# Fused dilated attention, Fourier mixing and FFN: five early FFN tiles, four weight tiles ahead, one key buffer, full-height transform matmuls

## The chip, the cores and the metric

One core of one Trainium2 chip. The time is the device time of one execution in microseconds (us); lower is better. The engines are TensorE (PE, with its weight loads shown apart as PEld), VectorE (DVE), ScalarE (ACT), GpSimd (POOL) and SyncE (SP, which issues most transfers).

## The reference

Attention over 8 batches of 576 tokens with 8 heads of 64, a causal window of 32 for half of the heads and a dilated one (every fourth key of 128) for the others; then a real Fourier mix over tokens and channels, a normalisation, and a two-layer FFN of 512 to 2048 to 512 with a residual.

```python
scores = scale * np.matmul(q, k.transpose(0, 1, 3, 2))
scores = np.where(masks[None], scores, -1e9)        # plain window / dilated window
attn = softmax(scores); x = np.matmul(attn, v)      # laid out as (8, 576, 512)
mixed = np.real(np.fft.fft(np.fft.fft(x, axis=1), axis=2))
u = x + mixed
un = (u - mean(u)) / np.sqrt(var(u) + 1e-6)
out = u + np.maximum(un @ w_ch1, 0.0) @ w_ch2       # float64 weights, 512x2048 and 2048x512
```

## The kernel before, in words

Every operation is recorded with a cost, a priority and the buffers that it touches (class `Plan`); a greedy list scheduler then writes each engine's instructions out in a fixed order. So an engine runs its list in order, and a number in the program can change the order everywhere.

- **Attention** (`attention`, `attend`): batch by batch, four pairs of heads each, three units a pair: scores (L536), mask and maximum on DVE (L544), exponent on ACT (L550), transposes (L563), values (L570). Queries and keys are transposed on DVE into `tq` and `tk` (L511), two buffers each; ACT copies `tk` into `kb` (L522).
- **Mix** (`mix`): the two transforms as matmuls with high and low parts: along the tokens (L752, its last piece with 97 or 33 rows in `eot` and `tail_sb`; the edge column at L774), along the channels (L798) with one matmul of 34 rows (`ye`, `alt_sb`, L804). Rows are normalised, written to DRAM (`us`) and read back transposed (`tokens`).
- **Weights** (`prep`): the float64 weights of one FFN tile f (128 of the 2048 hidden units) come as two loads, and DVE (L874 to L883, four instructions a load), ACT and POOL (L886) make high and low float32 parts of them. The first NF1 tiles (`wa`) are made during attention and staged in the ring `ut` of NUT = 3 buffers, in which the transposed token blocks also live and in which buffers are given out in the order of the program text: all `wa` stages stand ahead of the first token block. When attention is over its memory is freed, and NFA more tiles (`wb`) are made through a ring `wst` of two; the others follow when the mix memory is freed.
- **FFN**: tokens go in 9 chunks of 512 (8 of the batches, one of left-over rows). `fill` does the first few tiles of a chunk **early**, while attention and mix of later batches run, in blocks of 256 tokens: up (L900, `ut`, 256 columns) for each tile, then down (L916), and the partial sum goes to DRAM (`part`). Before the change chunks 0 to 8 have 4, 4, 4, 4, 3, 3, 3, 2, 0 early tiles. When the mix is done, the **late loop** runs chunk by chunk over the remaining tiles with 512 columns: 24 matmuls a tile, 12 up and 12 down (`utwbb` and `utlate` are its token blocks, `hh` its hidden values, whose low part DVE makes at L908).

Priorities: attention comes first, then mix, then weight tiles (8 + 8f), and `fill` last (1000 and more), so early tiles are what TensorE does when it has nothing else.

Of the kernel before, what the change touches and what calls it, by code (L numbers as in the profile page):

```python
# [9 lines left out]
F32 = mybir.dt.float32  # L10
# [9 lines left out]
P = 128  # L20
KT = C // P
NF = FF // P
NF1 = 4
N4 = 4
N2 = 1
TOK = 4 * P
TOK1 = 2 * P
NX = 4
NUT = 3
NUC = 2  # L30
NH = 4
NLATE = 4
NPE = 1
LO1 = 'DVE'
NFA = 2
P_QK0, P_V0 = -8.0, -7.0
P_ST, P_FD, P_WD, P_ST0, P_FD0, P_SPAN0, P_SPAN1 = -4.0, -12.0, -10.0, 0.0, 0.0, 8.0, 13.0
P_QK, P_V, P_TR, P_MIX, P_SPAN, P_W, P_WF, P_FILL, P_FILLT = -8.0, -7.0, -5.0, 2.0, 13.0, 8.0, 8.0, 45.0, 4.0
# [24 lines left out]
def tables():  # L63
    def split(t):
        hi = round12(t)
        return np.stack([hi, round12(t - hi)], axis=1).astype(np.float32)

    def turn(a, b, n, kind):
        k = np.outer(np.arange(a), np.arange(b)) % n
        ang = 2.0 * np.pi * k / n  # L70
        if kind == "cos":
            t = np.cos(ang)
            t[(4 * k == n) | (4 * k == 3 * n)] = 0.0
        else:
            t = np.sin(ang)
            t[(k == 0) | (2 * k == n)] = 0.0
        return t

    def pad(t, rows, cols):
        out = np.zeros((rows, cols))  # L80
        out[: t.shape[0], : t.shape[1]] = t
        return out

    seq = np.stack([split(pad(turn(NSH, NSH, S, kd), 3 * P, NSP)) for kd in ("cos", "sin")])
    seq = seq.reshape(2, 3, P, 2, NSP)
    tail = np.zeros((P, 3, NSP), np.float32)
    for r in (0, 64):
        tail[r:r + 33, 0] = seq[0, 2, :33, 0]
    for r in (64, 96):
        tail[r:r + 32, 1] = seq[1, 2, :32, 0]  # L90
    tail[0:33, 2] = seq[0, 2, :33, 1]
    tail[32:64, 1] = seq[1, 2, :32, 1]
    seq = seq[:, :2]
    ch = np.stack([split(pad(turn(2 * P, NEH, C, kd), 2 * P, NEP)) for kd in ("cos", "sin")])
    ch = ch.reshape(2, 2, P, 2, NEP)
    alt = np.zeros((34, NEP), np.float32)
    sign = 0.5 * (1.0 - 2.0 * (np.arange(NEH) % 2))
    for r in (0, 1, 32, 33):
        alt[r, :NEH] = sign
    q = np.arange(QB)[:, None]  # L100
    j = np.arange(KB)[None, :]
    band = (j > q) & (j <= q + WIN)
    first = band & (j >= WIN)
    cross = band & ((q < 48) | (j >= WIN + 48))
    mask = np.where(np.stack([band, first, cross], 1), 0.0, NEG).astype(np.float32)
    eye = np.eye(P, dtype=np.float32)
    rest = np.arange(P).reshape(4, 32)
    rest[1::2] = rest[1::2, ::-1]
    ident = np.stack([eye, eye[:, ::-1], eye[:, rest.reshape(-1)]], axis=1)
    n = np.arange(QB)  # L110
    orders = (
        np.concatenate([n[:72], n[:71:-1]]),
        np.concatenate([n[47::-1], n[48:]]),
        np.concatenate([n[:24], n[:23:-1]]),
    )
    perm = np.stack([eye[:QB, o] for o in orders], axis=1)
    flip = np.arange(P, dtype=np.int32)[::-1].reshape(P, 1)
    flip = np.concatenate([flip, rest.reshape(P, 1).astype(np.int32)], axis=1)
    flip = (flip[:, :, None] + P * np.arange(4, dtype=np.int32)).reshape(P, 8)
    return dict(  # L120
        seq=np.ascontiguousarray(seq),
        tail=tail,
        chn=np.ascontiguousarray(ch),
        alt=alt,
        mask=np.ascontiguousarray(mask),
        ident=np.ascontiguousarray(ident),
        perm=np.ascontiguousarray(perm),
        flip=np.ascontiguousarray(flip),
    )
# [211 lines left out]
def fused_kernel(ctx: ExitStack, tc, q, k, v, w1, w2, seq, tail, chn, alt, mask, ident, perm, flip, out):  # L341
# [30 lines left out]
    def attw(tag, shape, dtype=F32, bufs=2):  # L372
        return plan.buf(lambda: pools["att"], tag, shape, dtype, bufs)
# [4 lines left out]
    def fixed(pool_, shape, dtype, name):  # L378
        return Buf(ap=pool_.tile(shape, dtype, name=name))
# [11 lines left out]
    tail_sb = fixed(keep, [P, 3, NSP], F32R, "tail_sb")  # L391
    eot = fixed(keep, [P, 2, NEH], F32R, "eot")
    chn_sb = [fixed(keep, [P, 2, 2, NEP], F32R, f"chn{i}") for i in range(2)]
    alt_sb = fixed(keep, [34, NEP], F32R, "alt_sb")
    ye = fixed(keep, [34, NSP], F32R, "ye")
    half = fixed(keep, [P, 1], F32, "half")
    kbs = [fixed(heads, [P, 2, WIN + S], F32, f"kb{i}") for i in range(2)]
    vts = [fixed(heads, [P, 4, 6, D + 1], F32, f"vt{i}") for i in range(2)]
# [10 lines left out]
    def start():  # L409
        dma(lambda: nc.sync.dma_start(out=mask_sb(), in_=mask), (), (mask_sb,), -9, QB * 3 * KB * 4)  # L410
        dma(lambda: nc.sync.dma_start(out=ident_sb(), in_=ident), (), (ident_sb,), -8, P * 3 * P * 4)
        dma(lambda: nc.sync.dma_start(out=perm_sb(), in_=perm), (), (perm_sb,), -7, QB * QB * 12)
        dma(lambda: nc.sync.dma_start(out=flip_sb(), in_=flip), (), (flip_sb,), 50, P * 32)

        def zero(t, eng, cost, fn, key=None, prio=-5.0):
            add(eng, cost, fn, (), ((t, key) if key is not None else t,), prio)

        zero(half, "DVE", 0.07, lambda: nc.vector.memset(half(), -0.5))
        for n, t in enumerate(kbs):
            for e in range(2):  # L420
                def clear(t=t, e=e):
                    ps = slice(64 * e, 64 * e + 64)
                    nc.vector.memset(t()[ps, 1 - e], 0.0)
                    nc.vector.memset(t()[ps, e, 0:WIN], 0.0)
                zero(t, "DVE", 0.8, clear, ("z", e), -6.0 + n)
        for i, t in enumerate(vts):
            def ones(t=t, i=i):
                nc.gpsimd.memset(t()[:, :, :, D:D + 1], 1.0)
                for blk in ((0,), (0, 3))[i]:
                    nc.gpsimd.memset(t()[0:WIN, :, blk, 0:D], 0.0)  # L430
            zero(t, "POOL", 1.0, ones)
        for t in xs + xtail:
            zero(t, "DVE", 0.07, lambda t=t: nc.vector.memset(t()[:, C:C + 1], 0.0), "pad")
        zero(eot, "DVE", 0.2, lambda: nc.vector.memset(eot().bitcast(F32)[32:64, 0], 0.0), ("gap", 0))
        zero(eot, "DVE", 0.2, lambda: nc.vector.memset(eot().bitcast(F32)[0:32, 1], 0.0), ("gap", 1))
        zero(ye, "DVE", 0.2, lambda: nc.vector.memset(ye().bitcast(F32), 0.0))
        for b in range(B):
            dma(lambda b=b: nc.sync.dma_start(
                out=xsm[b]()[0:1], in_=kbs[0]()[0:1, 1, WIN:WIN + C],
            ), ((kbs[0], ("z", 0)),), ((xsm[b], "zero"),), 12 * b + 6, 2048)  # L440
        for i in range(2):
            for m in range(2):
                add("POOL", 0.06, lambda i=i, m=m: nc.gpsimd.dma_start(out=seq_sb[i]()[:, m], in_=seq[i, m]),
                    (), ((seq_sb[i], m),), 6 + i, P * 2 * NSP * 4, at=T_SEQ + i)
                add("POOL", 0.06, lambda i=i, m=m: nc.gpsimd.dma_start(out=chn_sb[i]()[:, m], in_=chn[i, m]),
                    (), ((chn_sb[i], m),), 9 + i, P * 2 * NEP * 4, at=T_CHN + i)
        add("POOL", 0.06, lambda: nc.gpsimd.dma_start(out=tail_sb(), in_=tail), (), (tail_sb,), 6.5, P * 3 * NSP * 4, at=T_SEQ + 0.5)
        add("POOL", 0.06, lambda: nc.gpsimd.dma_start(out=alt_sb(), in_=alt), (), (alt_sb,), 8, 34 * NEP * 4, at=T_SEQ + 4)

# [49 lines left out]
    def attend_pair(b, dil, j, staged, xts, when):  # L501
        p0 = when(0) + P_TR

        def transposed(name):
            t = attw("t" + name, [P, S])

            def go():
                o = t()[:, :]
                if dil:
                    o = t().rearrange("p (r n a) -> p n a r", r=DIL, n=18, a=8)  # L510
                nc.vector.transpose(  # L511
                    out=o, in_=staged[name]()[:, 18 * j:18 * j + 18].rearrange("p n d -> p (n d)")
                )
            add("DVE", 0.67, go, (staged[name],), (t,), p0)
            return t

        tq = transposed("q")
        kb = kbs[j]
        tk = transposed("k")
        for e in range(2):  # L520
            ps = slice(64 * e, 64 * e + 64)
            add("ACT", act(S), lambda e=e, ps=ps: nc.scalar.copy(out=kb()[ps, e, WIN:], in_=tk()[ps]),  # L522
                (tk,), ((kb, e),), p0)
        for u in range(3):
            attend(b, dil, j, u, tq, kb, xts[u], when(u))
# [145 lines left out]
    def mix(b, when):  # L671
# [59 lines left out]
        def pieces(i):  # L731
# [5 lines left out]
            def tail_of(cols):  # L737
                if i:
                    return [(eot()[:, 1, cols], tail_sb()[:, 1])]
                return [(eot()[r, 0, cols], tail_sb()[r, c]) for r, c in ((slice(0, 97), 0), (slice(0, 33), 2))]  # L740
            return [(((src, m),), (seq_sb[i], m), 3, whole(m)) for m in range(2)] + [
                (((eot, "eo"[i]), (eot, ("gap", i))), tail_sb, 2 - i, tail_of)]

# [296 lines left out]

    def early(c):

        if c == NCH - 1:
            return 0
        return NF1 if c < N4 else NF1 - 2 if c >= B - N2 else NF1 - 1

    def fill(ut, tiles):
        prio = P_FILL + tiles[0] * P_FILLT
# [113 lines left out]
```

## Time and profile before

| | |
|---|---|
| median of 3 runs | 1205.33 us (1204.33 to 1207.46) |
| the profiled execution | 1203.13 us, span 1201.4 us |
| TensorE clock granted, mean over the span | 0.975 of full |
| PE / DVE / ACT / POOL busy | 1119.6 / 638.5 / 456.1 / 298.5 us |
| matmuls | 5932 |
| transfers | 132.83 MB, mean 111 GB/s |

The span runs from the first to the last instruction; the profiled execution lasts 1.7 us longer than its span. Busy times of different engines overlap. A matmul of one group overlaps the next, so its mean duration is longer than the distance from one start to the next, and work is costed below by that distance.

### The profile page before, as it was taken

The page shows a single profiled execution, that of the slowest core. Times are in us where ns is not written, and L with a number is a line of the kernel's source. Part 1 is how long each engine was busy: PE and PEld are TensorE (multiplying, and loading weights), DVE is VectorE, ACT ScalarE, POOL GpSimd, SP SyncE. Part 2 cuts the span into 40 slices and gives each one's busy share as a digit, 9 for nine tenths or more (in the row PEclk, how much of TensorE's full clock was granted, in tenths as well). Part 3 has the DMA queues.
Part 4 walks back from the last instruction along what each step waited for, and adds up shares of the span by engine and source line. Part 5 has one row for each costly group of instructions (what it writes and reads, how often), then busy time and mean ns, then how long its engine had stood idle before and what let it go on. Part 6 is the DMA issues. An engine that isn't in the chain of part 4 may idle for free.

```text
span 1201.4 us, 17217 instructions
## 1 busy us (share of the span) xinstructions
PE 1119.6 (93%) x5932; PEld 917.6 (76%) x5932; DVE 638.5 (53%) x1993; ACT 456.1 (38%) x1036; POOL 298.5 (25%) x351
## 2 busy tenths in 40 slices
PE   3887999998999899988889999999999999999998
PEld 2666877787888787866767888888888888888886
DVE  4798888979886868759952231314132231411211
ACT  3785767667574735334332120212112121211210
POOL 1135454544333344414431010202001020110100
PEclk9788899999999999989899999999999999999999
DMA  9978869997777345463642130504031050400201
GB/s 204 218 172 155 165 147 158 219 168 149 155 176 158 91 115 183 123 201 123 173 124 72 38 103 1 141 1 123 18 88 53 2 139 1 123 18 1 88 1 36
DMA packets 284183, 132.83 MB, mean 111 GB/s; under 512 B 204998, under 2 KB 255528, under 8 KB 284096
## 3 DMA queue, kind: packets, MB, share of 16 engines
q1 hardware_dynamic: 280752, 123.22, 45.1%
q0 software_dynamic: 2960, 7.99, 2.4%
q8 instruction: 47, 0.77, 0.3%
q10 hardware_dynamic: 384, 0.52, 0.1%
q14 instruction: 40, 0.33, 0.1%
HBM read 94.94 MB, written 36.75 MB: 110 GB/s over the span
## 4 chain that ended last, share of the span: by engine, by line
PE 67%; DVE 14%; DMA 7%; SPq 4%; issue 3%; POOL 2%; ACT 2%; DVEq 0%; ACTq 0%; POOLq 0%
PE ff L900 26%; PE mix L916 9%; PE sc L916 8%; PE sc L536 4%; PE pt L916 4%; PE av L916 4%; DMA ut<-us 4%; PE av L570 3%; PE mix L752 3%; DVE ut L1007 2%; PE mix L798 2%; PE pt L563 2%; SPq L492 1%; DVE pm L544 1%; SPq L997 1%
## 5 line engine op out<-in xcount | busy, mean ns | idle before, releaser
L908 DVE SCALAR_TENSOR_TENSOR hh<-ff,hh 128x512 fp32r<-128x512 f32 x117 | 80.5, 688 | 389.6 <-ACT hh L906 389.6
L906 ACT ACTIVATE hh<-ff 128x512 fp32r<-128x512 f32 x117 | 69.8, 597 | 379.1 <-PE ff L900 378.8
L900 PE MATMUL ff<-utwbb,wb 128*128 128x512 f32 x720 | 181.0, 401 | 9.8 <-POOL wb L886 7.3
L900 PEld LDWEIGHTS ff<-utwbb,wb 128*128 128x128 f32 x720 | 138.8, 194 | 42.7 <-POOL wb L886 8.7
L550 ACT ACTIVATE pm<-pm,mx 96x128 f32<-96x128 f32 x384 | 132.0, 394 | 44.6 <-DVE mx L544 41.7
L900 PE MATMUL ff<-utlate,wb 128*128 128x512 f32 x576 | 139.9, 392 | 0.0
L536 PE MATMUL sc<-kb,tq 128*96 128x256 f32 x384 | 112.0, 408 | 22.9 <-ACT kb L522 20.6
L960 POOL DMA_INDIRECT ut<-us,flip_sb x20 | 19.5, 975 | 449.3 <-DMA out_dram<-ut 347.6
L900 PEld LDWEIGHTS ff<-utlate,wb 128*128 128x128 f32 x576 | 108.1, 188 | 24.2
L916 PE MATMUL sc<-wb,hh 128*128 128x512 f32 x432 | 111.9, 392 | 4.1 <-DVE hh L908 4.1
L916 PE MATMUL mix<-wb,hh 128*128 128x512 f32 x432 | 110.8, 391 | 0.3 <-DVE hh L908 0.2
L544 DVE CUSTOM_DVE_ANT_0 pm<-sc,mask_sb 96x128 f32<-96x128 f32 x384 | 94.5, 276 | 20.7 <-PE sc L536 15.4
L570 PEld LDWEIGHTS av<-vt,ptsb 128*96 128x96 f32 x768 | 79.7, 172 | 25.8 <-issue 7.1
L916 PEld LDWEIGHTS sc<-wb,hh 128*128 128x128 f32 x432 | 80.8, 188 | 23.6 <-DVE hh L908 5.7
L570 PE MATMUL av<-vt,ptsb 128*96 128x65 f32 x768 | 85.7, 256 | 11.6 <-DVE xt L582 8.7
L916 PEld LDWEIGHTS mix<-wb,hh 128*128 128x128 f32 x432 | 81.0, 188 | 18.6 <-DVE hh L908 0.5
L536 PEld LDWEIGHTS sc<-kb,tq 128*96 128x96 f32 x384 | 58.3, 177 | 35.0 <-ACT kb L522 20.8
L900 PE MATMUL ff<-ut,wa 128*128 128x256 f32 x528 | 80.3, 297 | 4.0 <-DVE h L908 4.0
L1007 DVE STREAM_TRANSPOSE ut<-ut 128x512 f32<-128x512 f32 (+1 forms) x68 | 66.6, 1020 | 32.1 <-DMA ut<-us 24.9
L900 PEld LDWEIGHTS ff<-ut,wa 128*128 128x128 f32 x528 | 70.5, 196 | 7.2 <-DVE h L908 4.8
L916 PE MATMUL ff<-wa,h 128*128 128x512 f32 x264 | 70.4, 407 | 0.7 <-ACT h L906 0.5
L916 PE MATMUL pt<-wb,hh 128*128 128x512 f32 x216 | 61.1, 391 | 0.0
(152 smaller groups left out, 1731.1 us busy)
## 6 DMA issues: line engine op xcount, KB each, us to landing
us<-uc SPq DMA_DIRECT2D x36, 257.0 KB
st<-in_q_dram SPq DMA_DIRECT2D x64, 144.0 KB
st<-in_k_dram SPq DMA_DIRECT2D x64, 144.0 KB
ut<-in_w_dram SPq DMA_DIRECT2D x18, 512.0 KB
ut<-us SPq DMA_DIRECT2D x36, 256.0 KB
part<-row SPq DMA_DIRECT2D x32, 256.0 KB
ut<-part SPq DMA_DIRECT2D x32, 256.0 KB
ut<-us SPq DMA_DIRECT2D x56, 128.0 KB
```

The source lines that it names most:

```text
L536: nc.tensor.matmul(sc()[:QB, 256 * n:256 * n + 256], lhsT=tq()[:, cols], rhs=kb()[:, :, keys], start=True, stop=True,)
L544: nc.vector.tensor_tensor_reduce(pm()[:, i], sc()[:QB, KB * i:KB * i + KB], mask_sb()[:, masks[blocks[i // 2]]], -0.125, 3.0e38, ALU.add, ...
L550: add("ACT", 0.295, lambda i=i: nc.scalar.activation(out=pm()[:, i], in_=pm()[:, i], func=AF.Exp, bias=mx()[:, i:i + 1], scale=-1.0), ((mx ...
L563: nc.tensor.transpose(ps()[:, QB * i:QB * i + QB], pm()[:, i], order)
L570: add("PE", 0.16, lambda i=i: nc.tensor.matmul(av()[:QB, 65 * i:65 * i + 65], lhsT=pt()[:, i], rhs=vts[dil]()[:, j + 2 * (i % 2), blocks[i ...
L752: nc.tensor.matmul(ps()[:, :NSP], lhsT=lt, rhs=tab, start=(m == 0 and n == 0), stop=(m == 2 and n == count - 1),)
L798: nc.tensor.matmul(ps()[:n, :NEP], lhsT=ys[i]()[:, dt, a, rows], rhs=chn_sb[i]()[:, dt, c], start=(dt == 0 and x == 0), stop=(i == 1 and d ...
L900: nc.tensor.matmul(z()[:, :n_tok], lhsT=wf()[:, a, kk], rhs=ut()[:, p, kk], start=(kk == 0 and n == 0), stop=(kk == KT - 1 and n == 2),)
L906: add("ACT", act(n_tok) - 0.05, lambda: nc.scalar.activation(out=h()[:, 0, :n_tok], in_=z()[:, :n_tok], func=AF.Relu), (z,), ((h, 0),), prio)
L908: add("DVE", dve(n_tok), lambda: nc.vector.scalar_tensor_tensor(h()[:, 1, :n_tok], z()[:, :n_tok], 0.0, h()[:, 0, :n_tok].bitcast(F32), op ...
L916: nc.tensor.matmul(acc(), lhsT=h()[:, a, P * s:P * s + P], rhs=wf()[:, p], start=(first and n == 0), stop=(last and n == 2),)
L1007: nc.vector.transpose(out=o[back], in_=x[:, g])
```

## The change

Chunks 0 to 8 get 5, 5, 5, 5, 4, 4, 4, 3, 0 early tiles (35 in place of 27). Five weight tiles instead of four are made during attention (NF1), with five buffers for hidden values (NH). Four instead of two further tiles are made after attention and before the mix memory is freed (NFA). `tk` has one buffer. `eot`, `ye`, `alt_sb` are used at their full 128 rows, with zeros in the rows that held nothing.

```diff
-NF1 = 4
-N4 = 4
-N2 = 1
+NF1 = 5
+NE = (5, 5, 5, 5, 4, 4, 4, 3, 0)
-NH = 4
+NH = 5
-NFA = 2
+NFA = 4
...
-    alt = np.zeros((34, NEP), np.float32)
+    alt = np.zeros((P, NEP), np.float32)
...
-    alt_sb = fixed(keep, [34, NEP], F32R, "alt_sb")
-    ye = fixed(keep, [34, NSP], F32R, "ye")
+    alt_sb = fixed(keep, [P, NEP], F32R, "alt_sb")
+    ye = fixed(keep, [P, NSP], F32R, "ye")
...
-        zero(eot, "DVE", 0.2, lambda: nc.vector.memset(eot().bitcast(F32)[32:64, 0], 0.0), ("gap", 0))
+        def gaps():
+            for r in (32, 96):
+                nc.vector.memset(eot().bitcast(F32)[r:r + 32, 0], 0.0)
+        zero(eot, "DVE", 0.4, gaps, ("gap", 0))
...
-            t = attw("t" + name, [P, S])
+            t = attw("t" + name, [P, S], F32, 2 if name == "q" else 1)
...
-                return [(eot()[r, 0, cols], tail_sb()[r, c]) for r, c in ((slice(0, 97), 0), (slice(0, 33), 2))]
+                return [(eot()[:, 0, cols], tail_sb()[:, c]) for c in (0, 2)]
...
-        if c == NCH - 1:
-            return 0
-        return NF1 if c < N4 else NF1 - 2 if c >= B - N2 else NF1 - 1
+        return NE[c]
```

Lines after the first edits are numbered 2 higher in the changed program (L900 is L902 there).

The change also moves the order of the engines' lists. First, TensorE's list of before around its first early up matmuls (`ff<-ut,wa_0` with 256 columns); 58 of the 192 score matmuls stand ahead of them.

```order
L651 MATMUL mix<-ident_sb,uc 128x128 x4
L570 MATMUL av<-vt_154,ptsb 96x65 x4
L536 MATMUL sc<-kb_153,tq 96x256
L563 MATMUL pt<-ident_sb,pm 128x96
L536 MATMUL sc<-kb_153,tq 96x256
L563 MATMUL pt<-ident_sb,pm 128x96 x2
L900 MATMUL ff<-ut,wa_0_132 128x256 x9
L563 MATMUL pt<-ident_sb,pm 128x96 x2
L900 MATMUL ff<-ut,wa_0_132 128x256 x3
L900 MATMUL ff<-ut,wa_1_133 128x256 x3
```

The same place of the change: TensorE's list around its first early up matmuls.

```order
L538 MATMUL sc<-kb_155,tq 96x256 x2
L653 MATMUL mix<-ident_sb,uc 128x128 x4
L572 MATMUL av<-vt_157,ptsb 96x65 x2
L653 MATMUL mix<-ident_sb,uc 128x128 x4
L572 MATMUL av<-vt_157,ptsb 96x65 x2
L565 MATMUL pt<-perm_sb,pm 128x96 x4
L538 MATMUL sc<-kb_155,tq 96x256 x2
L565 MATMUL pt<-perm_sb,pm 128x96 x4
L902 MATMUL ff<-ut,wa_0_132 128x256 x3
L572 MATMUL av<-vt_157,ptsb 96x65 x4
```

72 of the 192 score matmuls stand ahead of the first early up matmul now, that is exactly three batches of attention. Up to the last score matmul of the third batch the list had 48 early up matmuls and 137 transform matmuls; it has 0 and 75 now. Up to the last value matmul of all (L570) it had 339 up and 168 down matmuls of the early tiles, and has 423 and 210; behind it stood 309 and 156, and stand 417 and 210.

Second, POOL's list of the change where it makes the low parts of the last early weight tiles (`wa_3`, second half, and both halves of `wa_4`; `t`, `ees`, `oos`, `eot` are those of the second batch's mix).

```order
L705 TENSOR_TENSOR t_1714<-xt_163,xt_162 33x257
L888 TENSOR_TENSOR wa_3_140<-ut,wa_3_140 128x512
L725 TENSOR_TENSOR eot<-ee,eot 33x257
L727 TENSOR_TENSOR eot<-oo,eot 32x256
L888 TENSOR_TENSOR wa_4_136<-ut,wa_4_136 128x512
L888 TENSOR_TENSOR wa_4_141<-ut,wa_4_141 128x512
L668 TENSOR_TENSOR x_158<-x_158,dm 128x257
```

In the list of before the second half of `wa_3` is the last of the early tiles and stands directly behind the same two `eot` rows. The two halves of `wa_4` now follow them, ahead of the rows in which a mix adds its result (`x`, `dm`).

Third, TensorE's list of before where the late loop begins (chunk 0, tiles 4, 5, 6, 7; `sc`, `pt`, `av` are its sums).

```order
L900 MATMUL ff<-utwbb,wb_4_6204 128x512 x3
L900 MATMUL ff<-utwbb,wb_5_6206 128x512 x3
L916 MATMUL sc<-wb_4_6205,hh 128x512 x6
L916 MATMUL pt<-wb_4_6205,hh 128x512 x3
L916 MATMUL av<-wb_4_6205,hh 128x512 x3
L900 MATMUL ff<-utwbb,wb_6_7215 128x512 x12
L916 MATMUL sc<-wb_5_6207,hh 128x512 x6
```

The same place of the change.

```order
L918 MATMUL sc<-wb_5_6380,hh 128x512 x6
L918 MATMUL pt<-wb_5_6380,hh 128x512 x3
L918 MATMUL av<-wb_5_6380,hh 128x512 x3
L902 MATMUL ff<-utwbb,wb_7_6383 128x512 x12
L918 MATMUL sc<-wb_6_6382,hh 128x512 x6
L918 MATMUL pt<-wb_6_6382,hh 128x512 x3
L918 MATMUL av<-wb_6_6382,hh 128x512 x3
L902 MATMUL ff<-utwbb,wb_8_6385 128x512 x12
L918 MATMUL sc<-wb_7_6384,hh 128x512 x6
L918 MATMUL pt<-wb_7_6384,hh 128x512 x3
L918 MATMUL av<-wb_7_6384,hh 128x512 x3
L902 MATMUL ff<-utwbb,wb_9_7628 128x512 x12
```

Before, tile 6 is the first that is made after the mix memory is freed, and it is the third of chunk 0; now that is tile 9, the fifth of chunk 0.

## Rows read from the trace of the kernel before

**Rows 1.** The page, busy time (share), instructions of each engine.
```profile
PE 1119.6 (93%) x5932; PEld 917.6 (76%) x5932; DVE 638.5 (53%) x1993; ACT 456.1 (38%) x1036; POOL 298.5 (25%) x351
```
**Rows 2.** Stages: length, then busy (instructions) by engine, clock, DMA, GB/s.
```profile
core 0: us, PE busy (x) PEld busy (x) DVE busy (x) ACT busy (x) POOL busy (x), PEclk, DMA share, GB/s
51.50:99.00 47.50, 37.71 (x231) 28.10 (x229) 41.02 (x185) 38.58 (x98) 15.07 (x16) 0.87 0.90 193
99.00:159.80 60.80, 56.10 (x387) 46.84 (x387) 51.03 (x206) 38.46 (x97) 29.57 (x39) 0.91 0.68 129
159.80:426.80 267.00, 250.49 (x1757) 210.03 (x1756) 221.68 (x980) 174.34 (x458) 106.16 (x147) 0.99 0.78 161
426.80:528.50 101.70, 94.26 (x599) 81.19 (x597) 72.28 (x180) 40.73 (x91) 40.90 (x53) 1.00 0.54 150
528.50:532.20 3.70, 1.42 (x5) 0.86 (x5) 2.88 (x3) 1.84 (x4) 0.00 (x0) 0.73 0.39 140
532.20:618.40 86.20, 74.61 (x289) 57.61 (x290) 75.87 (x99) 35.59 (x61) 44.01 (x29) 0.91 0.48 147
618.40:1195.70 577.30, 577.02 (x2521) 472.76 (x2519) 143.44 (x202) 100.79 (x167) 53.63 (x47) 1.00 0.21 57
```
**Rows 3.** Timeline of PE, one early block: start, us, instructions.
```profile
508.64 1.58 PE L900 MATMUL av<-ut,wa 128*128 128x256 f32 x12
510.06 1.65 PE L900 MATMUL pt<-ut,wa 128*128 128x256 f32 x12
511.55 4.36 PE L916 MATMUL sc<-wa,h 128*128 128x512 f32 x18
515.75 1.58 PE L900 MATMUL pt<-ut,wa 128*128 128x256 f32 x12
```
**Rows 4.** Waits of PE from 524 to 640 us: total, times, longest.
```profile
PE ff L900 <- POOL wb L886: 7.3, 3, 4.7
PE sc L916 <- DVE hh L908: 4.1, 4, 3.0
```
**Rows 5.** Timeline of PE, chunk 0 of the late loop, with idle time before.
```profile
532.20 8.32 PE L900 MATMUL ff<-utwbb,wb 128*128 128x512 f32 x24 [2.28 <-ACT utwbb L1024]
...
573.44 4.89 PE L900 MATMUL ff<-utwbb,wb 128*128 128x512 f32 x11 [4.68 <-POOL wb L886]
...
586.37 2.88 PE L900 MATMUL ff<-utwbb,wb 128*128 128x512 f32 x12
...
608.70 4.37 PE L900 MATMUL ff<-utwbb,wb 128*128 128x512 f32 x11 [2.01 <-POOL wb L886]
```
**Rows 6.** The page's groups: count, busy us, mean ns, idle before.
```profile
L908 DVE SCALAR_TENSOR_TENSOR hh<-ff,hh 128x512 fp32r<-128x512 f32 x117 | 80.5, 688 | 389.6 <-ACT hh L906 389.6
```
**Rows 7.** Timeline of PE in the last mix, short and full last pieces.
```profile
467.82 1.38 PE L752 MATMUL mix<-tail_sb,eot 97*128 97x290 f32 x4
469.13 1.67 PE L916 MATMUL ff<-wa,h 128*128 128x512 f32 x6
...
473.71 0.97 PE L752 MATMUL mix<-seq,oos 128*128 128x290 f32 x6
474.52 0.30 PE L752 MATMUL mix<-tail_sb,eot 128*128 128x290 f32 x1
```
**Rows 8.** Groups of PE by shape, the short ones.
```profile
L752 PE MATMUL mix<-tail_sb,eot 97*128 97x290 f32 x16 | 6.6, 410 | 1.6 <-POOL eot L723 1.4
L804 PE MATMUL mix<-alt_sb,ye 34*128 34x258 f32 x16 | 6.1, 383 | 0.0
```
**Rows 9.** Groups of PEld by shape, the same piece at full and short height.
```profile
L752 PEld LDWEIGHTS mix<-tail_sb,eot 128*128 128x128 f32 x16 | 3.0, 190 | 0.0
L752 PEld LDWEIGHTS mix<-tail_sb,eot 97*128 97x128 f32 x16 | 3.0, 190 | 3.6 <-POOL eot L723 2.4
```
**Rows 10.** Timeline of PE, the first early up matmuls.
```profile
125.88 2.01 PE L900 MATMUL ff<-ut,wa 128*128 128x256 f32 x9
```
**Rows 11.** Timeline of POOL, the last early weight tile done.
```profile
151.24 1.28 POOL L886 TENSOR_TENSOR wa<-ut,wa 128x512 fp32r<-128x512 f32 x1 [8.62 <-ACT wa L885]
```
**Rows 12.** Groups of ACT by shape, copies out of the key buffer.
```profile
L522 ACT COPY kb<-tk 64x576 f32<-64x576 f32 x64 | 42.8, 669 | 28.7 <-DVE tk L511 18.5 <-DVE rinv L581 3.9 <-DVE sums L578 2.5
```

More of the change, by code (lines that the diff above doesn't have):

```diff
@@ L447, in start @@
         add("POOL", 0.06, lambda: nc.gpsimd.dma_start(out=tail_sb(), in_=tail), (), (tail_sb,), 6.5, P * 3 * NSP * 4, at=T_SEQ + 0.5)
-        add("POOL", 0.06, lambda: nc.gpsimd.dma_start(out=alt_sb(), in_=alt), (), (alt_sb,), 8, 34 * NEP * 4, at=T_SEQ + 4)
+        add("POOL", 0.06, lambda: nc.gpsimd.dma_start(out=alt_sb(), in_=alt), (), (alt_sb,), 8, P * NEP * 4, at=T_SEQ + 4)
     def load_v(b, dil, prio):
```

## The prediction

> **What bounds the kernel now.** The page's first part comes first: TensorE is busy in 93% of the span and no other engine in more than 53% [rows 1]. An average over stages hides where the rest is, so the next view is the table of stages [rows 2]. Its first two stages lie in attention (before 51.5 us stand the start and the first batch), the third ends with the scores of the last batch, the fourth with the last early tile, then come chunk 0 of the late loop and chunks 1 to 8. In the last stage TensorE is busy for 577.0 of 577.3 us at full clock, so nothing but TensorE sets its length: 105 tiles, 5.50 us each. Chunk 0 is another matter: 12 tiles take 86.2 us in place of 66.0, at a clock of 0.91, while VectorE is busy for 75.9 us. Between 159.8 and 528.5 us TensorE has 344.7 of 368.7 us. The waits near chunk 0 [rows 4] name POOL's weight parts (7.3 us) and VectorE's low parts of the hidden values (4.1 us), and the timeline [rows 5] shows where: the first up matmuls run cold (8.32 us for 24, in a stage after one at clock 0.73), the fifth tile that is made there waits 4.68 us, the tenth 2.01 us.
>
> **Tiles moved from late to early.** Eight chunk-tiles go from the late loop (117 to 109) to the early blocks (27 to 35). Late, one costs 5.50 us (above). Early, 12 up matmuls of 256 columns start 1.42 us after one another and 18 down matmuls take 4.20 us, 0.233 each [rows 3]; a block of 256 tokens needs 12 up and 6 down for a tile, 2.82 us, and a chunk two blocks, 5.64 us. So 45.1 us are added before 528.5 us and 44.0 us taken away after it: **+1.1 us**. That halving the columns nearly halves the time is what makes the move free, and also what makes it worthless by itself: the early phase is bound by TensorE as well, so it becomes longer by about what the late loop loses. By the counts of the order, 84 up and 42 down of these land before the end of attention, 108 and 54 behind it.
>
> **Chunk 0 of the late loop.** Ten tiles were made after the mix memory was freed, seven are now, and four instead of two stand ready. VectorE's 75.9 us there, less 11 low parts of 0.69 us [rows 6], leave 68.3 us for ten tiles (and four short transposes), 6.8 a tile, with 5.50 on TensorE: the tile that VectorE makes can't keep up with the one that TensorE eats, and the lead decides. Before, the fifth made tile was ready 41.2 us after the start at 532.2, the seventh no later than 54.2, the tenth after 76.5 [rows 5]. Now the first up needs 2.9 us extra for the cold clock as before, and the fifth made tile is wanted after 2.9 + 8 x 5.5 = 46.9 us, the seventh and last after 57.9. Both are there, by 5.7 and 3.7 us. So of 20.2 us lost (86.2 - 66.0) the cold start stays and some 2 us of small waits: 5 left, **-15 us**. Bounds: all but the cold start goes, -17; or VectorE is late for the last three tiles by what it was late for the last three before, and the gain is 8.
>
> **Two more tiles ahead, one more early.** Their VectorE work, 6.8 us a tile, goes into 426.8 to 528.5 us (two) and into attention (one). In the former VectorE is idle for 29.4 us and that stage grows by 25 us of early tiles, so TensorE covers it; without the cover the two would cost 13.6 us. Their loads meet DMA at 0.54 there, and SP's list is not what that stage waits for. **+1 us** for hidden values queued behind them on VectorE (0 to 6).
>
> **Full-height matmuls.** In the last mix [rows 7] four short pieces take 1.31 us to the next start, 0.33 each, while six full ones of the same 290 columns take 0.81 us, 0.135 each. The short one also spoils the next: the six down matmuls behind it take 1.67 us. There are 16 pieces of 97 rows and 16 of 33, and 16 + 8 channel matmuls of 34 rows [rows 8], besides 16 edge pieces of one column. 32 x 0.19 is 6.2 us; the 24 lose about 0.18 (wide ones last 0.08 us longer than full pieces of 290 columns, for 32 columns less) and as much as half of that behind them, 6 us; the edge some 1.5. That is 14 us at most on TensorE, of which part lies in stalls that stay: **-12 us**, 5 to 14. What the extra rows hold is zero, and the table that grows by 94 rows is loaded once.
> The weight loads themselves do not differ: 190 ns at 97 rows and at 128 [rows 9]. The Trainium skill, "TensorE: Matmul & The Clock Gate", section "LDWEIGHTS (loading the stationary operand)", says just this, that a load's time goes by columns and not by the contracted rows; the trace agrees, and by that rule alone padding would give nothing. The Trainium skill, "TensorEngine Tiling (Array Packing)", section "Key Properties", says on the other hand that a change of tiling mode, not of the tile alone, drains TensorE; the trace looks like that [rows 7], since the cost is in the distance between starts. I go by the distance.
>
> **The start of the early tiles.** This is the price. The ring of three `ut` buffers is given out in the order of the program, all weight stages first, so a fifth early tile stands between the ring and the first token block, with a later priority than attention's third batch. Before, the first early up ran at 125.88 us [rows 10], the last early tile being ready only after 151.24 us [rows 11]; now 14 more score matmuls go ahead of it, those that ran up to 159.8. By the order 48 up and 62 transform matmuls leave the stretch 99.0 to 159.8 us: 48 x 0.118 + 62 x 0.135 = 14.0 us of TensorE. Attention without that work is not paced by TensorE: in the stretch ahead one batch took 47.5 us with TensorE busy 37.7 at clock 0.87 and VectorE 41.0. A little over half of the transforms stay, so the stretch shrinks from 60.8 not to 47.5 but to about 54.5. 14.0 us of work are put off and 6.3 us come back: **+8 us**. Bounds 0 (it shrinks by all of it) and 14 (not at all).
>
> **One buffer of transposed keys.** The second pair's transpose waits until ACT has copied the first pair's, two copies of 0.67 us [rows 12]. In the order other VectorE work stands between them for most pairs. If VectorE stood still 1.3 us each of 16 times that would be 21 us, but VectorE has 45 us of idle time in the long stage of attention and TensorE has early tiles to run: **+1 us**, 0 to 5.
>
> **Sum** against the profiled execution: 1203.1 + 1.1 - 15 + 1 - 12 + 8 + 1 = 1187.2. The median shown is 2.2 us above that execution, so the forecast is 1189.
>
> **Rivals.**
> - *The stock fills the gaps.* Between 159.8 and 426.8 us TensorE is idle for 16.5 us; with more early tiles at hand half of it is filled, and the late start costs nothing because the same backlog is worked off there. 1189 - 8 - 8 = 1173. Against it: the list is fixed beforehand, and its gaps are mostly short waits on attention's own chain.
> - *Padding gives nothing*, because the distances [rows 7] come from other waits than height: 1189 + 12 = 1201. The rule of the LDWEIGHTS section named above would give this.
> - *Chunk 0 stays late.* VectorE, with seven tiles, 11 low parts and transposes in 65 us, still sets the pace and 5 us of the 15 come: 1199.
> - *Slower: the ring starves TensorE.* If the transforms queue behind token blocks that have no buffer, attention runs alone for longer. In 51.5 to 99.0 us a batch leaves TensorE idle 9.8 us, and about 6 more go to the half clock (0.13 of 47.5 us): 16 us a batch. Two batches' worth, 32 us in place of 8, gives 1213. It decides from about 28 us. For it speaks the order (no early up before the third batch's scores), against it that by the sixth batch's scores the list has overtaken the old one.
>
> **How the numbers follow.** Forecast, 1180 to 1197: 0.52. Gaps filled: 0.20. No padding gain: 0.09. Chunk 0 late: 0.06. Starved: 0.11. The remaining 0.02 is left open. What a measurement here can tell is 0.3%, 3.6 us, so faster means below 1201.7. Faster: 0.52 + 0.20 + most of the next two, 0.80; the rest of these and mild starvation make 0.09 for no change, 0.11 for slower. The range goes from the first rival to the edge of no change: 1173 to 1203.
>
> **What would show it.** The first early up at 150 us or later, with the stretch to the third batch's scores 5 to 8 us shorter; the late loop beginning near 571 us instead of 532; chunk 0 in about 66 us for 11 tiles, with under 2 us waited for POOL's weight parts; last pieces 0.135 us apart; chunks 1 to 8 in 539 us. I am wrong if chunk 0 still has waits of several us in its last tiles, if TensorE has idle slices between the second and fourth batch that the old page had not, or if the padded pieces keep their distance.

## The result and the profile after

| | before | after |
|---|---|---|
| median | 1206.24 us (1204.33 to 1207.46, 4 runs) | 1193.64 us (1192.72 to 1194.07, 4 runs) |
| span of the profiled execution | 1201.4 us | 1191.0 us |
| clock granted, mean | 0.975 | 0.977 |
| start of the late loop (first `utwbb` matmul) | 532.2 us | 572.2 us |
| chunk 0 of the late loop | 86.2 us, 12 tiles | 73.4 us, 11 tiles |
| chunks 1 to 8 and the end | 583.0 us, 105 tiles | 545.4 us, 98 tiles |

The ratio is 0.991, interval 0.989 to 0.9931: faster by 8 to 13 us (12.6 between the medians), forecast 16 to 17. In the profile: 40.0 us later into the late loop, then 12.8 us saved in chunk 0 and 37.6 us behind it.

The table of stages of the changed kernel (length, busy time and instructions by engine, clock, DMA share, GB/s), cut at the same events as [rows 2] where it can be:

```profile
142.50:438.60 296.10, 285.02 (x2055) 248.01 (x2056) 240.49 (x1041) 189.03 (x498) 110.31 (x155) 0.99 0.73 148
438.60:572.20 133.60, 121.45 (x765) 106.52 (x763) 94.71 (x207) 49.68 (x112) 49.52 (x57) 0.99 0.48 133
572.20:645.60 73.40, 64.30 (x264) 50.32 (x265) 56.55 (x74) 28.54 (x49) 31.19 (x23) 0.98 0.46 140
645.60:1185.30 539.70, 538.97 (x2353) 441.69 (x2351) 138.87 (x196) 95.76 (x159) 53.60 (x47) 1.00 0.22 60
```

The last stage is as full as before: 98 tiles in 539.7 us, 5.51 us each. Chunk 0 takes 12.9 us more than 11 tiles of 5.50 us. In 9.1 us of it TensorE does nothing; the other 3.8 us it is busy longer than these tiles need at full clock. Who is waited for is in the waits of TensorE from 566 to 650 us (total, times, longest; the 1.2 us for ScalarE's `utwbb` end where chunk 0 begins):

```profile
PE sc L918 <- DVE hh L910: 6.8, 4, 2.7
PE ff L902 <- ACT utwbb L1026: 1.2, 1, 1.2
PE sc L918 <- ACT hh L908: 1.2, 1, 1.2
PE ff L902 <- POOL utwbb L1029: 0.9, 2, 0.6
```

Against [rows 4]: the wait for POOL's weight parts (7.3 us) is gone, and that for VectorE's low parts of the hidden values has grown from 4.1 to 6.8 us. VectorE's timeline at the longest of them (start, length) and TensorE's beside it:

```profile
614.61 1.51 DVE L876 TENSOR_SCALAR ut<-ut 128x512 uint32<-128x512 uint32 x1
616.04 0.68 DVE L879 SCALAR_TENSOR_TENSOR wst<-wst 128x512 uint32<-128x512 uint32 x1
616.64 0.68 DVE L879 SCALAR_TENSOR_TENSOR ut<-ut 128x512 uint32<-128x512 uint32 x1
617.24 0.68 DVE L882 SCALAR_TENSOR_TENSOR wst<-wst 128x512 uint32<-128x512 uint32 x1
617.84 0.68 DVE L882 SCALAR_TENSOR_TENSOR ut<-ut 128x512 uint32<-128x512 uint32 x1
618.45 3.00 DVE L1009 STREAM_TRANSPOSE ut<-ut 128x512 f32<-128x512 f32 x3
621.37 0.65 DVE L910 SCALAR_TENSOR_TENSOR hh<-ff,hh 128x512 fp32r<-128x512 f32 x1
```

```profile
616.26 2.88 PE L902 MATMUL ff<-utwbb,wb 128*128 128x512 f32 x12
618.98 0.39 PE L918 MATMUL sc<-wb,hh 128*128 128x512 f32 x1
622.07 1.43 PE L918 MATMUL sc<-wb,hh 128*128 128x512 f32 x5 [2.71 <-DVE hh L910]
```

The low part that TensorE wants at 619.4 us stands in VectorE's list behind weight instructions and three transposes of the next chunk.

The start of chunk 0, up to the end of its first 36 matmuls, as a stage and in TensorE's timeline:

```profile
572.20:587.40 15.20, 11.33 (x36) 7.71 (x37) 10.93 (x16) 6.90 (x13) 7.65 (x6) 0.89 0.68 230
581.14 0.50 PE L918 MATMUL sc<-wb,hh 128*128 128x512 f32 x1 [1.23 <-ACT hh L908]
583.22 2.44 PE L918 MATMUL sc<-wb,hh 128*128 128x512 f32 x5 [1.58 <-DVE hh L910]
```

At full clock 36 matmuls take 8.2 us (36 x 0.229). TensorE is busy for 11.3 us here, 3.1 us more, at a granted clock of 0.89, and idle for 3.9 us. Before, the same 36 took 11.7 us, almost without a wait.

The last pieces at full height, in the timeline of TensorE of the changed kernel:

```profile
477.84 0.80 PE L754 MATMUL mix<-tail_sb,eot 128*128 128x290 f32 x4
478.48 1.71 PE L902 MATMUL ff<-ut,wa 128*128 128x256 f32 x13
...
487.50 0.28 PE L806 MATMUL mix<-alt_sb,ye 128*128 128x258 f32 x1
487.64 1.71 PE L800 MATMUL mix<-chn,y 128*128 128x258 f32 x12
```

Four pieces take 0.64 us to the next start, 0.16 each, against 0.33 in [rows 7]; the channel matmul lasts 0.28 us and the next starts 0.14 us after it has started.

### The profile page after: what moved, and what is told of

Read it like the earlier page. It is cut to its first block, busy times and chain, and to the rows that moved or that the text cites. A ratio compares the mean times of both kernels' runs of the same rounds, so it can differ in the third digit from the quotient of the medians.

```text
span 1191.0 us, 17444 instructions
## 1 busy us (share of the span) xinstructions
PE 1106.7 (93%) x6028; PEld 922.4 (77%) x6028; DVE 640.9 (54%) x2002; ACT 453.9 (38%) x1044; POOL 296.3 (25%) x351
## 4 chain that ended last, share of the span: by engine, by line
PE 65%; DVE 16%; DMA 7%; issue 4%; SPq 3%; POOL 2%; ACT 2%; DVEq 0%; ACTq 0%; POOLq 0%
PE ff L902 24%; PE mix L918 8%; PE sc L918 8%; PE sc L538 4%; PE pt L918 4%; PE av L918 4%; PE av L572 4%; DMA ut<-us 3%; PE ff L918 2%; PE mix L800 2%; DVE pm L546 2%; DVE ut L1009 2%; PE pt L565 2%; PE mix L754 2%; SPq L494 1%
## 5 line engine op out<-in xcount | busy, mean ns | idle before, releaser
L902 PE MATMUL ff<-utwbb,wb 128*128 128x512 f32 x660 | 161.0, 393 | 2.3 <-ACT utwbb L1026 1.2
L902 PEld LDWEIGHTS ff<-utwbb,wb 128*128 128x128 f32 x660 | 123.7, 188 | 31.0 <-POOL utwbb L1029 2.3
L902 PE MATMUL ff<-utlate,wb 128*128 128x512 f32 x528 | 127.8, 392 | 0.0
L902 PEld LDWEIGHTS ff<-utlate,wb 128*128 128x128 f32 x528 | 99.2, 188 | 21.8
L918 PE MATMUL sc<-wb,hh 128*128 128x512 f32 x396 | 103.6, 396 | 8.0 <-DVE hh L910 6.8
L902 PE MATMUL ff<-ut,wa 128*128 128x256 f32 x672 | 98.0, 294 | 7.4 <-DVE h L910 2.9
L918 PE MATMUL mix<-wb,hh 128*128 128x512 f32 x396 | 101.6, 392 | 0.7 <-DVE hh L910 0.7
L902 PEld LDWEIGHTS ff<-ut,wa 128*128 128x128 f32 x672 | 87.5, 193 | 10.3 <-DVE h L910 4.1
L918 PE MATMUL ff<-wa,h 128*128 128x512 f32 x336 | 85.7, 405 | 2.5 <-DVE h L910 1.8
L918 PEld LDWEIGHTS ff<-wa,h 128*128 128x128 f32 x336 | 62.6, 192 | 16.0 <-DVE h L910 2.0
```

The source lines that it names most:

```text
L902: nc.tensor.matmul(z()[:, :n_tok], lhsT=wf()[:, a, kk], rhs=ut()[:, p, kk], start=(kk == 0 and n == 0), stop=(kk == KT - 1 and n == 2),)
L918: nc.tensor.matmul(acc(), lhsT=h()[:, a, P * s:P * s + P], rhs=wf()[:, p], start=(first and n == 0), stop=(last and n == 2),)
```

## The experiments

All comparisons are ratios to runs of the kernel before on the same chip. The start of the late loop differs between profiled executions in which TensorE has the same list up to there: 572.2, 570.4, 572.2 and 572.9 us for four of the changed list, but 531.9 and 520.8 us for two of the padded old list, 11 us apart. So verdicts on a few us rest on medians, and a few us between the starts of two executions prove nothing.

**Padding alone.** The kernel before with the edits to `alt`, `alt_sb`, `ye`, `eot`, `tail_of`, and planned costs as they were:

```diff
-        zero(eot, "DVE", 0.2, lambda: nc.vector.memset(eot().bitcast(F32)[32:64, 0], 0.0), ("gap", 0))
+        zero(eot, "DVE", 0.2, gaps, ("gap", 0))
```

> The kernel before with the full-height transform matmuls and nothing else; the costs that the scheduler sees are kept, so that every engine's list is in the old order. My forecast (the distance between starts falls from 0.33 to 0.16 us for the last pieces): 5 to 14 us faster than before, 12 likeliest, most of it lost again only where TensorE waits anyway. Rival (a weight load goes by columns, so height is free): 0 us, within 0.3%.

1197.34 us, ratio 0.9918 (0.9891 to 0.9946): 10 us faster, 7 to 13 by the interval. Its runs spread from 1188.50 to 1202.71, and the profiled one is the longest, with the late loop at 531.9 us; it shows no gain by itself. Another run of the same list up to there (the padding with real costs, below) starts it at 520.8.

**The change without padding.** The same edits undone in the changed kernel, with the planned costs left as they are there:

```diff
-                return [(eot()[:, 0, cols], tail_sb()[:, c]) for c in (0, 2)]
+                return [(eot()[r, 0, cols], tail_sb()[r, c]) for r, c in ((slice(0, 97), 0), (slice(0, 33), 2))]
```

> The changed kernel with the short matmuls of before, all lists in the order of the changed kernel. If padding is worth what the forecast says wherever it is put, this is 12 us slower than the changed kernel (5 to 14), about 0.999 of before, and the rest of the change is worth next to nothing. Rival: padding is worth nothing, and this stays at 0.99 of before.

1202.21 us, ratio 0.9983 (0.9967 to 0.9999). Everything but padding is worth 2 us. Chunk 0 takes 73.4 us as in the changed kernel, and the late loop begins at 585.7 us: padding took 13.5 us off the way there in these two executions, 9 us between the medians (0.9983 to 0.991 of 1205). Both comparisons of medians agree. The Trainium skill's rule that a weight load's time goes by its columns, whatever the rows ("TensorE: Matmul & The Clock Gate", section "LDWEIGHTS (loading the stationary operand)"), by which padding would give nothing, does not price this matmul. What the short piece loses is not a longer load but the overlap: the trace of this run from 165.3 to 166.6 us, first the weight loads (PEld), then the matmuls.

```profile
165.35 0.19 PEld L751 LDWEIGHTS mix<-tail_sb,eot 97*128 97x128 f32 x1
165.71 0.18 PEld L751 LDWEIGHTS mix<-tail_sb,eot 33*128 33x128 f32 x1 [0.17 <-issue]
166.04 0.70 PEld L751 LDWEIGHTS mix<-seq,ees 128*128 128x128 f32 x5
165.08 0.57 PE L751 MATMUL mix<-seq,ees 128*128 128x290 f32 x3
165.48 0.62 PE L751 MATMUL mix<-tail_sb,eot 97*128 97x290 f32 x2
166.04 0.81 PE L751 MATMUL mix<-seq,ees 128*128 128x290 f32 x4
```

The load of the 97-row piece starts 0.13 us ahead of its matmul, and that matmul follows the full ones at their own distance, 0.13 us. The load of the 33-row piece starts only with its matmul, at 165.71, and so does the load of the full piece behind it, at 166.04, 0.33 us later. So it is the change between 33 rows and 97 or 128 that costs, not the 97 rows.

**Two tiles ahead instead of four.**

```diff
-NFA = 4
+NFA = 2
```

> The changed kernel with two instead of four tiles made before the mix memory is freed (nine are made after it). The lists are the same up to there. Forecast's theory (the lead decides): chunk 0 waits for POOL's weight parts again as before, chunk 0 takes some 81 us instead of 73.4, and the run is 7 to 10 us slower than the changed kernel (about 0.998 of before). Rival (VectorE's list sets the pace of chunk 0 whatever the lead): less than 3 us slower.

1193.44 us, ratio 0.9907 (0.9887 to 0.9927): the same as the change. The waits for POOL's weight parts are back, but those for the low parts shrink, in the waits of TensorE from 565 to 646 us:

```profile
PE ff L902 <- POOL wb L888: 4.7, 1, 4.7
PE sc L918 <- DVE hh L910: 2.2, 3, 1.7
```

Chunk 0 takes 77.0 us, 3.6 more, and the late loop begins at 569.1 us, 1 to 4 earlier than in the four executions with four ahead. The medians say that the two tiles paid before the loop what they saved in it.

**Light weight tiles.** Tiles 9 to 15 with one VectorE instruction a load for four; their values are not the weights', so only the time is read:

```diff
+        if lite:
+            add("DVE", 0.6, lambda: nc.vector.scalar_tensor_tensor(
+                bits(F32), mag(), F64_MIN, mag(), op0=ALU.is_ge, op1=ALU.mult), (m,), (v,), prio)
```

> The changed kernel, in which the weight tiles that are made after the mix memory is freed (9 to 15) are made with one VectorE instruction a load instead of four; their values are not those of the weights, so only the time is read. TensorE's list is the same. Theory: what is left of chunk 0's loss (12.9 us of 73.4) is VectorE's low parts of hidden values queued behind its slow weight instructions; then the waits for them (6.8 us) go, chunk 0 takes 64 to 67 us, and the run is 6 to 9 us faster than the changed kernel. Rival: the loss is the cold start and the transfers of the weights; then less than 3 us come.

1189.03 us, ratio 0.9863 (0.9844 to 0.9883). Chunk 0 takes 68.1 us, the waits for low parts fall from 6.8 to 2.1. So 5.3 of the 12.9 us lost in chunk 0 are VectorE's weight work ahead of the low parts; 7.6 are not. The expected 64 to 67 us was too low, since most of those 7.6 lie in the first 36 matmuls: they still take 14.2 us here.

**The fifth tile staged later.** First chunk with 4 early tiles, and:

```diff
-    for f in range(NF1):
+    for f in range(NF1 - 1):
         prep_w(f, wa1[f], wa2[f], utb, (), P_W + P_WF * f)
     for b in range(B):
+        if b == 1:
+            prep_w(NF1 - 1, wa1[NF1 - 1], wa2[NF1 - 1], utb, (), P_W + P_WF * (NF1 - 1))
```

> The changed kernel with 4 instead of 5 early tiles in the first chunk, and the fifth weight tile staged behind the first batch's token blocks. The first early up then has 58 score matmuls ahead of it as before the change, not 72. Theory (the ring holds back the first token blocks, and TensorE loses time that it gives back nowhere): the late loop begins 8 us earlier than that of the changed kernel beside the 5.6 us of the tile that is left out (near 558 instead of 572), and the run is 6 to 10 us faster than the changed kernel, about 0.984 of before. Rival (the backlog is worked off in gaps that are there anyway): within 3 us of the changed kernel.

1189.48 us, ratio 0.9892 (0.987 to 0.9913), against 0.991 for the change: 2 us, within the noise. The first early up runs at 121.7 us and the late loop begins at 562.6 us, 9.7 earlier, 5.6 of which are the tile left out; the rest, 4 us, is half of what was expected. Chunk 0 takes 81.3 us for its 12 tiles, so it lost 15.3, more than the change's 12.9.

**Weights due sooner.**

```diff
-P_QK, P_V, P_TR, P_MIX, P_SPAN, P_W, P_WF, P_FILL, P_FILLT = -8.0, -7.0, -5.0, 2.0, 13.0, 8.0, 8.0, 45.0, 4.0
+P_QK, P_V, P_TR, P_MIX, P_SPAN, P_W, P_WF, P_FILL, P_FILLT = -8.0, -7.0, -5.0, 2.0, 13.0, 8.0, 5.0, 45.0, 4.0
```

> The changed kernel with weight tiles due every 5 instead of every 8 units of the planner's priority, so that all five are made sooner and 56 score matmuls stand ahead of the first early up. The tiles are those of the changed kernel. Theory of the late start: 4 to 8 us faster than the changed kernel, since VectorE's weight work now delays the second batch of attention a little. Rival: within 3 us, or slower, because attention pays for it.

1198.11 us, ratio 0.9955 (0.9937 to 0.9973): 5 us slower than the change. The first early up comes at 130.9 us, 17 us sooner, but the last score of the third batch starts at 164.9 us in place of 147.6 and the late loop at 579.3: an earlier start of the early tiles is no gain when attention pays for it. My theory had the sign wrong here, and the rival had it right.

**Two key buffers.**

```diff
-            t = attw("t" + name, [P, S], F32, 2 if name == "q" else 1)
+            t = attw("t" + name, [P, S])
```

> The changed kernel with two buffers of transposed keys again; much of the order in attention differs. My term for the single buffer was 1 us (0 to 5): this run is within 3 us of the changed kernel, not more than 5 us faster. Rival: the one buffer holds attention up, and 5 us or more come back.

1190.65 us, ratio 0.9905 (0.9878 to 0.9931): no difference that can be told. The order of attention differs too, so the buffer alone is not isolated; it costs no more than some 4 us.

**Real costs for the late weight tiles.** Only the order changes:

```diff
-        prep_w(f, wb1[f], wb2[f], stage, (gate1, gate2) if late else (gate1,), FILL + f)
+        prep_w(f, wb1[f], wb2[f], stage, (gate1, gate2) if late else (gate1,), FILL + f, 1.6 if late else 1.0)
```

> The changed kernel with VectorE's instructions on the weight tiles of chunk 0 planned at 1.6 times their cost (0.54 and 0.96 us, about what the trace shows there), so that the low parts of the hidden values stand earlier in VectorE's list; no work is changed. Theory (TensorE waits 6.8 us in chunk 0 because the low parts are queued behind more weight instructions than was planned): 3 to 5 us of these waits go, chunk 0 takes 68 to 70 us, 3 to 5 us faster than the changed kernel. Rival: the weights come later in their turn and TensorE waits for them instead; within 2 us.

1189.79 us, ratio 0.9899 (0.9879 to 0.9919). Chunk 0 takes 69.8 us, 3.6 less, and the waits of TensorE from 568 to 645 us have all but lost the low parts:

```profile
PE sc L918 <- ACT wb L887: 1.6, 1, 1.6
...
PE sc L918 <- DVE hh L910: 0.5, 2, 0.2
```

The waits that it was to remove are gone in the trace; between medians (0.9899 and 0.991) the gain is not told from nothing.

**The change again,** unchanged, on the chip of the next three.

> The changed kernel once more, on the chip of the three runs beside it and with more rounds. The effects found so far (padding 8 to 13 us, the two further tiles 0) say 0.991 of before, within 0.002.

1192.97 us, ratio 0.9912 (0.9892 to 0.9931), late loop at 570.4 us, chunk 0 in 73.4.

**Both together:** the fifth tile staged later, with the real costs.

> The fifth weight tile staged behind the first blocks (first chunk with 4 early tiles) and the real costs of the late weight tiles, together. If the two gains (2 to 4 us before the late loop, 3.6 us in chunk 0) are of different stages and both real, they add: 5 to 7 us faster than the changed kernel in the same comparison, about 0.985 of before. Rival: they are noise of the order and this is within 2 us of the changed kernel.

1183.11 us, ratio 0.9829 (0.9806 to 0.9851), 10 us faster than the change on the same chip and 20 us faster than before: the best version here. More than the sum of both: with the real costs chunk 0 takes 72.2 us for 12 tiles, 9.1 less than in the fifth tile's experiment, and TensorE is at full clock in it (the stage in the fifth tile's experiment, then in this kernel):

```profile
562.50:643.80 81.30, 74.06 (x288) 58.04 (x289) 57.68 (x75) 29.40 (x50) 32.08 (x23) 0.92 0.41 126
563.00:635.20 72.20, 67.99 (x289) 53.78 (x290) 54.66 (x75) 28.43 (x49) 30.23 (x22) 1.00 0.45 135
```

Of the 9.1 us, 6.1 are time that TensorE is busy less for the same tiles, at a clock of 1.00 in place of 0.92, and 3.0 are idle time. That shorter waits kept the clock up was not tested.

**Padding and real costs in the kernel before,** ten tiles made late.

> The kernel before with full-height matmuls and the real costs of its ten late weight tiles; no tile is moved and none made further ahead. Theory (order and speed of VectorE's list set chunk 0, not the lead): chunk 0 takes 79 to 83 us instead of 86.4, and the run is 3 to 7 us faster than padding alone, about 0.988 of before, equal to the whole change within 3 us. Rival (the lead decides): ten tiles at 6.8 us remain too slow, chunk 0 stays at 85 us or more.

1200.13 us, ratio 0.9966 (0.995 to 0.9983): slower than padding alone. Chunk 0 takes 91.1 us, worse than 86.4. The rival's outcome came. The waits for weights fell, from 7.4 to 4.5 us, but a new one is the largest from 516 to 612 us:

```profile
PE sc L919 <- ACT hh L909: 6.2, 8, 1.4
```

With the weights planned later, TensorE's list sets the down matmuls of many a tile directly behind its own up matmuls, so TensorE stands still, mostly for 0.69 us and then 0.23 us, until ScalarE and VectorE have made the hidden values that it has just computed.

**Two ahead with real costs.**

> The changed kernel with two tiles ahead and the real costs. The two tiles moved into the stage before the late loop made that stage 3.1 us longer and chunk 0 3.6 us shorter. With the list in the real costs: if the lead is worth something of its own, chunk 0 here stays at 76 us or more while four ahead gave 69.8; if not, it takes 70 to 73 us and the run is within 2 us of four ahead with real costs (0.990 of before).

1196.34 us, ratio 0.9939 (0.9922 to 0.9955). The late loop begins at 563.9 us. The first matmuls of chunk 1 stand ahead of chunk 0's last down matmuls here:

```profile
642.16 0.73 PE L902 MATMUL ff<-utlate,wb 128*128 128x512 f32 x2 [0.55 <-ACT utlate L1026]
643.52 0.50 PE L902 MATMUL ff<-utlate,wb 128*128 128x512 f32 x1 [0.62 <-POOL utlate L1029]
643.86 0.40 PE L918 MATMUL sc<-wb,hh 128*128 128x512 f32 x1
...
648.63 4.96 PE L902 MATMUL ff<-utlate,wb 128*128 128x512 f32 x21
```

So chunk 0 ends at 648.6 us, and with those three matmuls takes 84.7 us where four ahead took 69.8. The largest wait is again that for ScalarE's hidden values, 8.1 us from 560 to 650 us. The two further tiles are worth some 14 us of chunk 0 in this list; 8 us of that they cost ahead of it (572.2 against 563.9), and 5 us of the whole are left between the medians. In the list as it was they gave nothing of the whole.

## Why the prediction was right, and where not

- **Tiles moved from late to early: right.** Chunks 1 to 8 give 5.51 us a tile. Without padding the late loop begins 53.5 us later, 45.1 of them the tiles; the move itself gains nothing.
- **What this costs before the loop: right as a sum, not settled in its parts.** 53.5 - 45.1 = 8.4 us, where I had 8 + 1 + 1 for the late start, the key buffer and the cover of further tiles. Since two executions of one list can differ by 11 us there, part of this agreement may be luck. The first early up came at 148.1 us, forecast 150 or later. The third batch (last score to last score) took 68.0 us before and 57.7 after, 62.5 without padding, so 5.5 us came back, 6.3 forecast. But staging the fifth tile later brought back 4 us of it, and two tiles fewer ahead 1 to 9 by six executions. The late start may be nearer to 4 than to 8 and the cover dearer than 1; neither is shown.
- **Padding: right in size, and in its cause but for the 97 rows.** 9 to 10 us in two comparisons of medians, in the range 5 to 14 and somewhat under 12. It is nearly the whole gain: the change without it is at 0.9983. I priced the pieces of 97 rows as short ones; they lose time only beside pieces of 33.
- **Chunk 0: the step that failed.** I forecast 20.2 us of loss falling to 5, a gain of 15; it fell to 12.9, a gain of 7.3. I asked when each weight tile is ready, and that part holds: no wait for POOL's weight parts is left. The cold start holds too: TensorE is busy 3.1 us longer than at full clock in the first 36 matmuls, where I had 2.9. The term that failed is the "some 2 us of small waits": TensorE is idle for 9.1 us, 6.8 of them for the low parts of the hidden values. I did not ask what else is queued on VectorE: they stand there behind weight instructions and transposes. With light tiles chunk 0 was 5.3 us shorter, with real costs 3.6.
- **The sum.** 1187.2 for the profiled execution, measured 1192.7 (the span 1191.0 and the 1.7 around it). By stages, the terms put the start of the late loop at 575.3 us (532.2 + 45.1 + 1 - 12 + 8 + 1; the 571 that was named as a sign is not what they add up to), and it came at 572.2, 3.1 us earlier. Chunk 0 took 7.9 us more than its 65.5, the rest 0.9 us more. The 3.1 us lie within what two executions of one list differ by.

Of the rivals, "chunk 0 stays late" is the one that came half true, by its own mechanism: VectorE sets the pace there. That padding gives nothing fell in two experiments, and the ring starved nobody. That early tiles fill attention's gaps came in part and without profit: TensorE was idle for 11.1 of 296.1 us in the long stage, less than the 16.5 of 267.0 before, but ahead of it, from 51.7 us on, for 19.8 of 90.8 us, more than the 14.5 of 108.3 before.

What stays open: how the 8.4 us before the loop divide, since each experiment on it reorders thousands of instructions and the start of the loop moves between executions of one list; and why the clock stays up in chunk 0 when later staging and real costs come together, which gives 10 us where the two alone give 1 and 2.

## What to carry to other kernels

Moving work off the last stage gains nothing when the stage that receives it is bound by the same engine; look for the edits that remove engine time, here matmuls whose number of contracted rows differed from their neighbours'. When a producer is given a lead, look at the list of the engine that makes it for what else stands there: the wait comes back under the next name. And a planner's wrong cost shows only when something waits behind it: the four VectorE instructions of a weight load were planned at 2.14 us, and in chunk 0 they last 3.4.

## What the runs showed of the hardware

Between a float32 matmul that contracts 33 or 34 rows and one of 97 or 128, in either order, TensorE's next weight load starts with its own matmul and not 0.12 to 0.13 us ahead of it. Such a matmul of 128 weight columns is followed by the next after 0.31 to 0.33 us, where full ones of the same columns stand 0.12 to 0.14 us apart; a load of 128 columns is recorded with 183 to 191 ns at any of these heights. A matmul of 97 rows behind one of 128 keeps the short distance, 0.13 to 0.14 us, in seven of the eight edge pieces before the change. The Trainium skill, "TensorEngine Tiling (Array Packing)", section "Key Properties", says that changing the tiling mode drains TensorE; that fits a cost at the change of height, but no run here shows the drain itself.

VectorE's shift instruction of 128x512 (L876) took 0.42 us and, at 614.61 us, 1.51 us, beside a POOL instruction on the same kind of tile. In the whole trace of the changed kernel 27 of the 128 VectorE instructions on weights (L876 to L885) last over 1 us, and all 27 overlap a POOL instruction on two tiles (TENSOR_TENSOR) in time; the 75 that overlap none last 0.70 us at most. That POOL is the cause was not tested.
